# A layernorm, gated MLP and FFT mixer on one core: a new opening order, a second buffer for the squares, and one more unit ahead on the first chunk

## The chip, the core and the metric

The kernel runs on one core of one Trainium2 chip. The time is the device time of one execution in microseconds; the kernel before has a median of 447.81 us over three runs (446.77 to 447.93). All traces are of one execution by the hardware profiler.

## The reference

Three terms are added: x itself, a 2-D Fourier filter of the normalised x, and a gated MLP of the same normalised x. Sizes: 2048 rows, 448 features, 1792 hidden features, all in float32.

```python
xn = (x - mean(x)) / sqrt(var(x) + 1e-5)                  # over the 448 features
A = irfft2(rfft2(xn) * (w_r + 1j * w_i), s=(2048, 448))
gate, up = xn @ W_gate, xn @ W_up                         # 448 x 1792
B = (gate * (gate > 0) * up) @ W_down                     # 1792 x 448
out = x + A + B
```

## The kernel before

Matrix products run in float16 pairs: every operand is split in a high and a low half, and a product is the sum of high-high, high-low and low-high passes. So each weight slab and each activation needs a conversion on ScalarE (`w_hi`, `ln_hi`, `gu_hi`: the high half) and a subtraction on VectorE (`w_lo`, `ln_lo`, `gu_lo`: the remainder). Before a slab (one of gate or up for 128 hidden features: f is the block of features, g is 0 or 1) is converted, it is scaled by a power of two: `w_sq` squares it with a running sum on ScalarE (L186), `w_sum` adds the sums over the partitions on GpSimd (L189), `w_scale` makes the exponent on VectorE (L192, L196), and then come `w_hi` (L681) and `w_lo` (L685). The squares' other output goes into a scratch tile named junk.

The rows of x are taken in 16 blocks of 128, numbered n2, and four blocks form a chunk q (n2 = q + 4 j). The chunks are worked in the order 0, 2, 1, 3. For chunk 0 the normalised blocks are transposed by TensorE (`ln_tp`, L332, with an identity matrix) and evicted into the tile T0 (`ln_ev`, on VectorE or ScalarE); for the others the DMA transposes them (`ln_dma`, L326). One gate/up unit is a pair (f, q): 20 matmuls of 512 columns (`gu_full`, L731), and a half pass for the 64 features that are left over (`gu_half`, L738). The half passes of two units, called mates, stand together in groups of four. A unit's sums are then taken through relu (`gu_relu`, ScalarE, L768), product (`gu_times`, VectorE, L772), `gu_hi` and `gu_lo`. PSUM has two buffers for units, so a unit can open when the product of the last but one is done. After all units of a group of five, five or four f on one chunk, four down products (`dn_mm`, L799) add up their part for its four blocks.

Meanwhile the Fourier transform runs as background work: a list `bg` of pieces, each with an estimated cost on VectorE, which a planner spreads over the units. `PE_US`, `fl`, `bf`, `il` and `V_US` hold the costs, `took` the length of a unit, `fixed` what a unit's own work costs VectorE, and `room` how much background a unit may take; the share is solved so that all fits. `t_ninth` copies leftover rows of T into the tile Tl (L348, L349), and the transform's first matmuls read both (`f_dft`, L361).

The first 45 us, called the opening, are not planned: the table `OPENING` names pieces in order, and each engine takes its part in that order. Of the names: lx and ly load a block of x, lw the next weight slab, lwd a slab of W_down, st, sq and rs make the statistics and the reciprocal root (A for blocks 0 and 4, B for 8 and 12, C for chunk 2), xn, hi, lo, cp normalise and split, tpA and tpB transpose, vev and aev evict, dm is a DMA transpose, wsq, par, wsc, whi, wlo prepare slabs, hh, lh, hl are unit 0's matmuls on half a chunk (256 columns), gu a slab's 20 or 10 matmuls, hp the half passes, re, tm, gh, gl a unit's way out, wd.. the same for W_down. warm and kw are pads: matmuls on a zeroed tile that do no work. All DMAs of this part are issued by SP in its order; SP waits with each for the landing of the one eight places before.

Of the kernel before, what the change touches and what calls it, by code (L numbers as in the profile page):

```python
# [25 lines left out]
NWARM = 19  # L26
# [4 lines left out]
lx0 lx4 lw lid lw lx8 lx12 lw lw lw lw lx2 lx10 lx6 lx14 lwd0 lwd1 lwd2 lwd3 lwd4 warm st0 st4 sqA rsA hi4  # L31
xn4 xn0 wsqW0g0 cp4 st8 hi0 parW0g0 st12 wsqW0g1 cp0 tpA0 lo0 tpA4 kw1 wscW0g0 sqB tpB0 kw6 parW0g1 wsqW1g0
rsB whiW0g0 vevB0 lo4 wsqW1g1 xn12 tpB4 kw3 hi8 parW1 wscW0g1 xn8 whiW0g1 cp8 vevA0 vevA4 hi12 tpA8 vevB4
hh10 hh00 lo8 wsqW2g1 cp12 tpA12 hl00 lo12 aevA12 tpB8 aevA8 hl10 wloW0g0 lw aevB8 tpB12 wscW1 lh00 aevB12
wloW0g1 lw lfd hh01 hh11 whiW1g0 st2 lh01 lh10 whiW1g1 hl01 wloW1g0 lw hl11 wsqW2g0 wloW1g1 lw ly0 ly4 ly8
ly12 lh11 wsqW3g0 st10 parW2 hp0 st14 wsqW3g1 gu1g0 st6 wdq0 parW3 wscW2 sqC wscW3 whiW2g0 rsC gu1g1 re0
wloW2g0 whiW3g1 tm0 whiW2g1 xn6 wsqW4g0 xn2 gu2g0 wloW2g1 hi2 re1 xn10 gh0 wloW3g1 whiW3g0 tm1 gu2g1 wdq1
wloW3g0 hi10 xn14 lo2 hi14 hi6 cp14 hp2 wsqW4g1 cp2 lo6 gu3g0 cp10 dm2 lo14 re2 parW4 wdq2 cp6 wscW4 tm2
whiW4g0 dm14 lo10 wdq4 gu3g1 wloW4g0 gh1 dm10 gl0 whiW4g1 gl1 dm6 gu4g0 re3 wloW4g1 wdq3 tm3 wdp gh3
wdsc gh2 gu4g1 gl2 wdh1 wdh2 wdl1 wdh0 wdl2 hp4 gl3 re4 wdh3 tm4 wdl0 gh4 wdh4 gl4 wdl3 wdl4  # L40
# [4 lines left out]
SQ = 2.0 ** -16  # L45
# [37 lines left out]
def _constants():  # L83
# [55 lines left out]
    ident = np.eye(128, dtype=np.float16)  # L139
    return dict(ident=ident, c_fd=c_fd, c_fm=np.ascontiguousarray(c_fm), c_im=c_im, c_row=c_row,  # L140
# [4 lines left out]
def tile_gfnet_reglu(ctx: ExitStack, tc: tile.TileContext, x, xr, wgu, wd, wf, ident, c_fd, c_fm, c_im, c_row, c_id,  # L145
# [39 lines left out]
    def squares(src, acc):  # L185
        A.activation(mt([128, 512], BF16, "junk")[:, 0:src.shape[-1]], src, AF.Square, scale=SQ, accum_out=acc)  # L186
# [18 lines left out]
    id_t = ft([128, 128], F16, "id_t")  # L205
# [10 lines left out]
    def load_xr(n2):  # L216

        xr_b[n2] = free.pop(0)
        xr_t[n2] = xr_b[n2].rearrange("p g c k -> p (g c k)")[:, 0:D]
        nc.sync.dma_start(xr_t[n2], xrv[:, n2, :])  # L220
# [36 lines left out]
    def ln_sd(q, js=(0, 1, 2, 3)):  # L257
        w = ft([128, 5, 4], F32, "rs", 3)
        n = len(js)
        rst[q, js[0]] = w[:, :, 0:n], mv[q][:, js[0]:js[-1] + 1, :]  # L260
        A.activation(w[:, 0, 0:n], rst[q, js[0]][1][:, :, 1], AF.Sqrt, bias=eps)

    def ln_rstd(q, js=(0, 1, 2, 3), bias=False):
        w, m = rst[q, js[0]]
        sd, r0, t, r, nm = (w[:, i] for i in range(5))
        V.reciprocal(r0, sd)
# [61 lines left out]
    def ln_tp(n2, tiles):  # L328
        if n2 not in tp:
            tp[n2] = fx().bitcast(F16).rearrange("p (a b) -> p a b", b=128)  # L330
        for a in tiles:
            P.transpose(tp[n2][:, a, :], tt[n2][:, a, :], id_t)  # L332
# [395 lines left out]
    def gu_full(f, q, gs, cs, start, stop, seq=SEQ):  # L728
        for g in gs:
# [4 lines left out]
    def gu_half(f, q, g, start, prev):  # L734
# [3 lines left out]
        m = P.matmul(hps[f, q][:, g, 0:512], wt[f, g][rows, 7, :], Tq[q][rows, b, :], start=start, stop=not start).ins  # L738
# [35 lines left out]
    def gu_hi(f, q):  # L774
        ht[f, q] = mt([128, 2, 512], F16, "h", NR + 2)
# [61 lines left out]
    PE_US = {"f_dft": 0.6, "f_sdft": 1.14, "i_sdft": 0.65, "i_ddft": 0.6, "row_dft": 0.2}  # L837
# [4 lines left out]
    def ln_chunk(q):  # L842
        for j in range(4):
            add(0.79, ln_stats, q, j)
# [3 lines left out]
        for t in range(4 + 2):  # L848
            for st, (c, fn) in reversed(list(enumerate(((0.0, ln_norm), (0.78, ln_lo), (0.0, ln_dma))))):
# [372 lines left out]
```

## Time and profile before

| | |
|---|---|
| median of 3 runs | 447.81 us (446.77 to 447.93) |
| the profiled execution | 447.5 us |
| its span, first to last instruction | 445.7 us |
| TensorE, VectorE, ScalarE, GpSimd busy | 438.1, 386.9, 187.0, 27.7 us |
| DMA, mean | 89 GB/s |
| first gate/up matmul | 14.36 us |
| first down matmul | 43.30 us |

In the rows of the profile, L731 is line 731 of the kernel, "out<-in" are tiles by the program's names without buffer numbers, and "x20" is a count. In the timeline the first number is the start in us, the second the length, and the brackets hold the idle time of the engine before it and who ended it. PEld is the loading of weights for TensorE, which overlaps its matmuls; SPq are DMA issues.

### The profile page before, as it was taken

What the parts mean: (1) busy time and instruction counts of PE and PEld (TensorE: products, weight loads), DVE (VectorE), ACT (ScalarE), POOL (GpSimd) and SP (SyncE); (2) the same over time, 40 slices, a digit from 0 to 9 for tenths busy, and PEclk for the clock granted to TensorE, in tenths of its full rate; (3) what the DMA queues carried; (4) which work ended last, traced back from release to release, by engine and by line L of the source; (5) the groups of instructions that cost most, each with busy time, mean ns of one, the idle gap of its engine ahead of it and who ended that gap; (6) DMA issues with size and microseconds to landing.
All of it is one profiled execution on the core that took longest, in us unless ns stands there. A gap on an engine that the chain in (4) does not pass through costs nothing.

```text
span 445.7 us, 7367 instructions
## 1 busy us (share of the span) xinstructions
PE 438.1 (98%) x2625; PEld 219.4 (49%) x2625; DVE 386.9 (87%) x958; ACT 187.0 (42%) x398; POOL 27.7 (6%) x77
## 2 busy tenths in 40 slices
PE   6999999999999999999999999999999999999997
PEld 2644645455445444444444444444454555555654
DVE  5999779786969999899999999999979799699753
ACT  4897263642552975133114354253323134144230
POOL 4220011200100040000000010000000000000000
PEclk9999999999999999999999999999999999999999
DMA  7919995400001272422220210002011211201212
GB/s 249 338 50 252 304 355 106 96 0 17 8 1 48 96 226 80 128 61 83 85 84 2 83 42 1 1 1 73 12 48 47 70 34 56 89 28 53 96 63 82
DMA packets 37756, 39.54 MB, mean 89 GB/s; under 512 B 16550, under 2 KB 33624, under 8 KB 37720
## 3 DMA queue, kind: packets, MB, share of 16 engines
q1 hardware_dynamic: 37720, 39.09, 28.3%
q8 instruction: 20, 0.33, 0.3%
q14 instruction: 16, 0.13, 0.1%
HBM read 24.38 MB, written 3.67 MB: 63 GB/s over the span
## 4 chain that ended last, share of the span: by engine, by line
PE 79%; DVE 9%; DMA 5%; ACT 3%; issue 1%; SPq 1%; DVEq 0%; ACTq 0%
PE gu L731 44%; PE dn L799 22%; PE gu L738 3%; PE fx L630 2%; PE fx L649 2%; PE fx L361 2%; PE fx L398 2%; DMA wf<-in_wf 1%; DMA sw<-y 1%; DMA y<-in_xr 1%; ACT junk L186 1%; PE dn L819 1%; ACT wt L681 1%; PE gu L819 1%; DVE wt L685 1%
## 5 line engine op out<-in xcount | busy, mean ns | idle before, releaser
L731 PE MATMUL gu<-T,wt 128*128 128x512 f16 (+1 forms) x1140 | 255.0, 375 | 0.0
L731 PEld LDWEIGHTS <-wt 128*128 128x128 f16 x1140 | 108.7, 98 | 128.7 <-issue 8.9
L799 PE MATMUL dn<-wdt,h 128*128 128x448 f16 x624 | 127.6, 353 | 0.1
L799 PEld LDWEIGHTS <-h 128*128 128x128 f16 x624 | 60.2, 98 | 57.7 <-issue 0.8
L768 ACT ACTIVATE g<-gu 128x512 f32<-128x512 f32 x56 | 33.0, 590 | 82.4 <-PE gu L738 55.6
L776 ACT ACTIVATE h<-g 128x512 f16<-128x512 f32 x56 | 35.1, 628 | 76.8 <-DVE g L772 73.8
L772 DVE SCALAR_TENSOR_TENSOR g<-gu,g 128x512 f32<-128x512 f32 x56 | 38.3, 684 | 4.2 <-ACT g L768 4.1
L780 DVE TENSOR_TENSOR h<-g,h 128x512 f16<-128x512 f32 x56 | 38.3, 685 | 3.7 <-ACT h L776 3.4
L805 DVE SCALAR_TENSOR_TENSOR xy<-dn,dsc,xy 128x448 f32<-128x448 f32 x44 | 29.9, 679 | 6.3 <-PE dn L799 6.2
L614 ACT ACTIVATE vt<-y,fsc 128x456 f16<-128x456 f32 x16 | 10.8, 673 | 26.1 <-PE fx L630 13.3
L654 DVE SCALAR_TENSOR_TENSOR xy<-fx,fsc,xy 128x448 f32<-128x448 f32 x16 | 10.8, 680 | 11.8 <-PE fx L649 11.7
L681 ACT ACTIVATE wt<-wst,wsc 128x512 f16<-128x512 f32 x28 | 19.2, 715 | 3.8 <-DVE wsc L196 3.8
L685 DVE SCALAR_TENSOR_TENSOR wt<-wst,wsc,wt 128x512 f16<-128x512 f32 x28 | 20.5, 747 | 0.1
L189 POOL PARTITION_ALL_REDUCE wm<-wm x15 | 7.8, 518 | 179.6 <-ACT junk L186 175.5
L186 ACT ACTIVATE junk<-wst 128x512 bf16<-128x512 f32 x28 | 17.5, 624 | 1.0 <-DMA wst<-in_wgu 0.7
L738 PE MATMUL gu<-T,wt 64*128 64x512 f16 x112 | 17.0, 381 | 0.2 <-DVE wt L685 0.2
L535 DVE TENSOR_TENSOR y<-y,sw 128x228 f32<-128x228 f32 x32 | 12.5, 390 | 5.0 <-DMA sw<-y 4.9
L405 DVE TENSOR_TENSOR y<-y,y 128x456 f32<-128x456 f32 x22 | 13.8, 629 | 1.7 <-DMA row<-y 1.4
L392 DVE TENSOR_TENSOR Xh<-X,Xh 128x456 f16<-128x456 f32 x16 | 10.0, 628 | 5.6 <-ACT Xh L389 5.5
L404 DVE TENSOR_TENSOR y<-y,y 128x456 f32<-128x456 f32 x22 | 13.9, 630 | 0.3
L389 ACT ACTIVATE Xh<-X 128x456 f16<-128x456 f32 x16 | 9.3, 578 | 10.1 <-DVE X L387 8.9
L630 PE MATMUL fx<-im,vt 128*128 128x128 f16 x192 | 13.4, 219 | 0.0
(130 smaller groups left out, 479.0 us busy)
## 6 DMA issues: line engine op xcount, KB each, us to landing
sw<-y SPq DMA_DIRECT2D x64, 112.2 KB
wst<-in_wgu SPq DMA_DIRECT2D x28, 256.0 KB
wf<-in_wf SPq DMA_DIRECT2D x16, 228.0 KB
y<-in_xr SPq DMA_DIRECT2D x16, 224.0 KB
xy<-in_x SPq DMA_DIRECT2D x16, 224.0 KB
out<-xy SPq DMA_DIRECT2D x15, 224.0 KB
wdst<-in_wd SPq DMA_DIRECT2D x14, 224.0 KB
fm<-in_c_fm SPq DMA_DIRECT2D x4, 256.0 KB
```

What stands on the lines that cost most here:

```text
L186: A.activation(mt([128, 512], BF16, "junk")[:, 0:src.shape[-1]], src, AF.Square, scale=SQ, accum_out=acc)
L630: P.matmul(o, v[:, h, w], m[:, c, :], start=(i == 0), stop=(i == 2), skip_group_check=True)
L681: A.activation(w[:, 0:4, :], wst[f, g], AF.Copy, scale=wsc[f, g])
L685: V.scalar_tensor_tensor(w[:, 4:8, :], st, sc, w[:, 0:4, :], op0=OP.mult, op1=OP.subtract)
L731: last["P"] = P.matmul(hps[f, q][:, g, cs], wt[f, g][:, a, :], Tq[q][:, b, cs], start=(start and i == 0), stop=(stop and i == len(seq) - 1 ...
L738: m = P.matmul(hps[f, q][:, g, 0:512], wt[f, g][rows, 7, :], Tq[q][rows, b, :], start=start, stop=not start).ins
L768: last["A"] = A.activation(g1s[f, q], hps[f, q][:, 0, :], AF.Relu, scale=2.0 ** -22).ins
L772: last["V"] = V.scalar_tensor_tensor(g1, hps[f, q][:, 1, :], 2.0 ** -22, g1, op0=OP.mult, op1=OP.mult).ins
L776: A.activation(ht[f, q][:, 0, :], g1s[f, q], AF.Copy)
L780: V.tensor_tensor(h[:, 1, :], g1s.pop((f, q)), h[:, 0, :], op=OP.subtract)
L799: last["P"] = P.matmul(ps[:, 0:D], ht[f, q][:, a, js], wdt[f][:, b, :], start=(i == 0), stop=(i == n - 1)).ins
L805: last["V"] = V.scalar_tensor_tensor(xy[:, n2, :], dps[n2][:, 0:D], dsc[:, g:g + 1], xy[:, n2, :], op0=OP.mult, op1=OP.add).ins
```

## The change

It rewrites the table of the opening, and what goes with it:

- The order. Four weight slabs instead of two are loaded ahead of x's third block, and slab W01 is squared first. The two transposed blocks of the second half come after the first matmuls of units 0 and 1. Unit 1 is also done in halves (ah, bh, ch).
- A sixth unit. The unit (f = 5, chunk 0) is taken out of the second group's place and done in the opening, as the mate of unit 4; its output has a tile of its own, h0, until the group's down product. The mates after it shift by one.
- The identity comes with block 4 in one load (`xi`), and the DMA of its own goes. The third block that TensorE transposes uses a PSUM buffer of the down products.
- The squares' scratch tile has two buffers.
- The root and the reciprocal become one function, Abs_reciprocal_sqrt, and VectorE's reciprocal goes.
- The pads: 15, 1, 8 and 1 instead of 19, 1, 6 and 3; VectorE clears their tile instead of GpSimd.
- The planner's costs are lower, and a unit whose fixed work exceeds its share passes the lack on to the units ahead of it (`rooms`). `c_fm` is loaded not before unit 6.

On ScalarE, at the start of the program, before. wst_124, 127, 131 and 133 are the slabs W00, W01, W10 and W11; L186 squares, L300 converts a block of x, L261 is the root, L681 scales a slab:

```order
L300 ACTIVATE tt0_103<-y1_71,rs_179 128x448
L186 ACTIVATE junk_190,wm_189<-wst_124 128x512
L300 ACTIVATE tt1_104<-y0_70,rs_179 128x448
L186 ACTIVATE junk_202,wm_189<-wst_127 128x512
L261 ACTIVATE rs_220<-mv_174,eps_95 128x2
L186 ACTIVATE junk_235,wm_234<-wst_131 128x512
L681 ACTIVATE wt_242<-wst_124,wsc_217 128x512
L186 ACTIVATE junk_247,wm_234<-wst_133 128x512
L300 ACTIVATE tt2_105<-y2_72,rs_220 128x448
L681 ACTIVATE wt_264<-wst_127,wsc_260 128x512
```

The same place now, with wst_159, 161, 165 and 167 for W00, W01, W10 and W11, and L685 for the scaling:

```order
L303 ACTIVATE tt0_102<-y0_70,rs_131 128x448
L305 ACTIVATE tt1_103<-y1_71 128x448
L186 ACTIVATE junk_176,wm_175<-wst_161 128x512
L186 ACTIVATE junk_191,wm_175<-wst_159 128x512
L186 ACTIVATE junk_196,wm_195<-wst_165 128x512
L186 ACTIVATE junk_198,wm_195<-wst_167 128x512
L685 ACTIVATE wt_211<-wst_161,wsc_207 128x512
L685 ACTIVATE wt_229<-wst_159,wsc_226 128x512
L342 ACTIVATE T0_62<-fx_171 128x5x128
L265 ACTIVATE rs_246<-mv_124,eps_95 128x2
```

The four squares now stand together ahead of all scalings, and the conversion of the third block of x has moved behind four scalings.

On ScalarE around the relu of unit 2 (L768 before, g1_513), before:

```order
L768 ACTIVATE g1_457<-gu_380 128x512
L776 ACTIVATE h_460<-g1_431 128x512
L681 ACTIVATE wt_463<-wst_311,wsc_412 128x512
L186 ACTIVATE junk_476,wdm_403<-wdst_145 128x448
L302 ACTIVATE tt1_104<-y14_84 128x448
L302 ACTIVATE tt2_105<-y15_85 128x448
L302 ACTIVATE tt3_106<-y12_82 128x448
L186 ACTIVATE junk_492,wm_440<-wst_364 128x512
L768 ACTIVATE g1_513<-gu_444 128x512
```

The same now (L776 is the relu, g1_446 that of unit 1 and g1_525 that of unit 2):

```order
L776 ACTIVATE g1_446<-gu_272 128x512
L265 ACTIVATE rs_461<-mv_359,eps_95 128x4
L186 ACTIVATE junk_464,wm_463<-wst_456 128x512
L186 ACTIVATE junk_466,wdm_392<-wdst_371 128x448
L685 ACTIVATE wt_472<-wst_368,wsc_469 128x512
L186 ACTIVATE junk_512,wm_463<-wst_458 128x512
L303 ACTIVATE tt0_102<-y8_78,rs_461 128x448
L776 ACTIVATE g1_525<-gu_474 128x512
```

Between the two relus now stand the squares of unit 5's slabs, the root of chunk 2 and one conversion, where three conversions of chunk 2 and unit 0's own way out stood; these follow later.

On SP, the transposes of chunk 2 (into T2) and the copies of chunk 0's leftover rows (into Tl0), before:

```order
L1056 DMA fd_t_101<-in_c_fd 128x912
L226 DMA wst_355<-in_wgu 128x512
L226 DMA wst_364<-in_wgu 128x512
L214 DMA xy_61<-in_x 128x448 x4
L326 DMA_TRANSPOSE T2_63<-tt0_103 128x8x128
L326 DMA_TRANSPOSE T2_63<-tt2_105 128x8x128
L326 DMA_TRANSPOSE T2_63<-tt1_104 128x8x128
L326 DMA_TRANSPOSE T2_63<-tt3_106 128x8x128
```

And now:

```order
L329 DMA_TRANSPOSE T2_63<-tt1_103 128x8x128
L329 DMA_TRANSPOSE T2_63<-tt2_104 128x8x128
L329 DMA_TRANSPOSE T2_63<-tt0_102 128x8x128
L213 DMA xy_61<-in_x 128x448
L329 DMA_TRANSPOSE T2_63<-tt3_105 128x8x128
L244 DMA fm_696<-in_c_fm 128x1024
L1067 DMA fd_t_100<-in_c_fd 128x912
L224 DMA y15_85<-in_xr 128x448
L224 DMA y16_86<-in_xr 128x448
L224 DMA y2_72<-in_xr 128x448
L224 DMA y1_71<-in_xr 128x448
L352 DMA Tl0_66<-T0_62 16x512 x3
```

A load of x now stands ahead of the last transpose, and the load of c_fd, which stood before all of them, has come between the transposes and the copies into Tl0.

The core of the diff:

```diff
-NWARM = 19
+NWARM = 15
 OPENING = """
-lx0 lx4 lw lid lw lx8 lx12 lw lw lw lw lx2 lx10 lx6 lx14 lwd0 lwd1 lwd2 lwd3 lwd4 warm st0 st4 sqA rsA hi4
...
+lx0 st0 lx4 st4 sqA rsA hi0 warm tpA0 xn4 xn0 lw lw lo0 lw lw hx4 kw1 tpA4 wsqW0g1 cp0 tpB0 lx8 lo4 lx12 cp4
...
-        A.activation(mt([128, 512], BF16, "junk")[:, 0:src.shape[-1]], src, AF.Square, scale=SQ, accum_out=acc)
+        A.activation(mt([128, 512], BF16, "junk", 2)[:, 0:src.shape[-1]], src, AF.Square, scale=SQ, accum_out=acc)
...
+        if n2 == 4:
+            t = mt([128, 512], F32, "g1", 3)
+            nc.sync.dma_start(t, xi)
+            xr_t[n2], state["id"] = t[:, 0:D], t[:, D:].bitcast(F16)
+            return
...
-        A.activation(w[:, 0, 0:n], rst[q, js[0]][1][:, :, 1], AF.Sqrt, bias=eps)
+        A.activation(w[:, 0, 0:n], rst[q, js[0]][1][:, :, 1], AF.Abs_reciprocal_sqrt, bias=eps)
...
-        V.reciprocal(r0, sd)
...
+            t = fx() if len(tp) != 2 else psum.tile([128, 512], F32, name="dn", bufs=2)
...
-        ht[f, q] = mt([128, 2, 512], F16, "h", NR + 2)
+        ht[f, q] = mt([128, 2, 512], F16, "h", NR + 2) if (f, q) != (NR, CHUNKS[0]) else mt([128, 2, 512], F16, "h0")
...
-    PE_US = {"f_dft": 0.6, "f_sdft": 1.14, "i_sdft": 0.65, "i_ddft": 0.6, "row_dft": 0.2}
+    PE_US = {"f_dft": 0.58, "f_sdft": 0.58, "i_sdft": 0.7, "i_ddft": 0.57, "row_dft": 0.1}
...
-    bf = (1.26, 2.04, 2.04, 2.04, 1.56, 2.04, 2.04, 2.04)
+    bf = (1.09, 1.71, 1.71, 1.71, 1.23, 1.71, 1.71, 1.71)
...
+    ahead = ("gu", 1, groups[1][0], CHUNKS[0])
+    gseq.remove(ahead)
+    gseq.insert(len(groups[0]), ahead)
...
-        sched(gus[5 + 2 * c], load_fm, q)
+        sched(max(gus[5 + 2 * c], len(groups[0]) + 1), load_fm, q)
...
-        A.activation(mt([128, 1], F32, "root"), eps, AF.Sqrt)
-        G.memset(warm, 0.0)
+        A.activation(mt([128, 1], F32, "root"), eps, AF.Abs_reciprocal_sqrt)
+        V.memset(warm, 0.0)
...
-    took = lambda u: 4.55 if u[0] == "gu" else 0.56 * len(groups[u[1]])
-    V_US = {"w_scale": 0.33, "w_lo": 0.75, "wd_scale": 1.5, "wd_lo": 0.68}
+    took = lambda u: 4.62 if u[0] == "gu" else 0.56 * len(groups[u[1]])
+    V_US = {"w_scale": 0.3, "w_lo": 0.67, "wd_scale": 1.4, "wd_lo": 0.59}
...
-        c = 1.37 if units[i][0] == "gu" else 0.68
+        c = 1.21 if units[i][0] == "gu" else 0.6
...
-    def room(i, share):
-        return max(0.0, share * took(units[i]) - fixed(i))
+    def rooms(share):
+        r, short = [0.0] * len(units), 0.0
+        for i in reversed(range(len(units))):
+            v = share * took(units[i]) - fixed(i) + short
+            r[i], short = max(0.0, v), min(0.0, v)
+        return r
```

More of the change, by code (lines that the diff above doesn't have):

```diff
@@ L732, in gu_full, with gu_half @@
                                      start=(start and i == 0), stop=(stop and i == len(seq) - 1)).ins
-    def gu_half(f, q, g, start, prev):
+    def gu_half(f, q, g, start, prev, stop):
         rows, b = TOP[g]
-        m = P.matmul(hps[f, q][:, g, 0:512], wt[f, g][rows, 7, :], Tq[q][rows, b, :], start=start, stop=not start).ins
+        m = P.matmul(hps[f, q][:, g, 0:512], wt[f, g][rows, 7, :], Tq[q][rows, b, :], start=start, stop=stop).ins
         if "opened" in state:
@@ L756, in gu_halves @@
     def gu_halves(f, q, mate):
-        gu_open(*mate)
+        fresh = mate not in hps
+        if fresh:
+            gu_open(*mate)
         m = last["P"]
@@ L1016, in gslot @@
         return gus[n] if n >= 0 else -1
-    for f in groups[1] + groups[2]:
+    for f in groups[1][1:] + groups[2]:
         s = first[f]
@@ L1028, in tile_gfnet_reglu @@
     for i in range(8):
-        sched(gslot(first[groups[1][0]], 14 - i // 2), load_wn)
+        sched(gslot(first[groups[1][1]], 14 - i // 2), load_wn)
     for c, q in enumerate(CHUNKS[1:]):
@@ L1136, in tile_gfnet_reglu @@
         need = sum(c - m * p for c, p, _, _ in bg)
-        lo, hi = (m, hi) if sum(room(i, m) for i in range(RAMP, last_gu)) < need else (lo, m)
+        lo, hi = (m, hi) if sum(rooms(m)[RAMP:last_gu]) < need else (lo, m)
     load[0] = hi
+    room = rooms(hi)
     anchors, act_anchors = [last["V"]], [last["A"]]
@@ L1145, in after @@
             yield
-    for i, u in list(enumerate(units))[len(groups[0]):-4]:
+    for i, u in list(enumerate(units))[len(groups[0]) + 1:-4]:
         is_gu = u[0] == "gu"
```

82 lines of the change are left out of this document (44 added, 38 removed).

## The prediction

> **What bounds the kernel now.** I read the page first (busy time by engine), then what TensorE waited for, then the chain of waits, and last the timeline of the first 50 us, where the change is.
>
> ```profile
> span 445.7 us, 7367 instructions
> PE 438.1 (98%) x2625; PEld 219.4 (49%) x2625; DVE 386.9 (87%) x958; ACT 187.0 (42%) x398; POOL 27.7 (6%) x77
> PE dn L1054 <- POOL warm L1111: 3.6, 1, 3.6
> PE fx L332 <- ACT wt L681: 0.5, 1, 0.5
> PE gu L738 <- DVE wt L685: 0.2, 1, 0.2
> 15.34 0.44 PE gu L731 x4
> 38.50 0.54 PE gu L738 x4
> 76.03 4.32 PE gu L731 x20
> ```
>
> The three PE rows with "<-" are all of TensorE's waits that the profile names: after 20 us it waits for nobody. The last three rows are pieces of the chain: a 256-wide gate/up matmul takes 0.44 / 4 = 0.109 us, a 512-wide one 4.32 / 20 = 0.216 us, a group of four half passes 0.54 us. So from about 20 us on the kernel is the plain sum of TensorE's stream. A change of order can win only by starting that stream earlier, or lose by new waits. The profiled execution took 447.5 us, 1.8 us beside its span of 445.7; the median of the runs is 447.81 us, 0.3 us above it.
>
> In the opening TensorE waits for ScalarE, which is nearly full:
>
> ```profile
> 10.00:20.00 10.00, 9.30 (x87) 6.65 (x86) 9.64 (x32) 9.17 (x20) 1.91 (x6) 1.00 0.96 357
> 20.00:30.00 10.00, 10.00 (x50) 4.14 (x47) 9.19 (x26) 9.32 (x23) 0.93 (x5) 1.00 0.29 94
> 13.39 0.72 ACT L681 ACTIVATE wt<-wst,wsc 128x512 f16<-128x512 f32 x1 [0.55 <-DVE wsc L196]
> 14.15 0.18 PEld L332 LDWEIGHTS <-tt 128*128 128x128 f16 x3 [0.95 <-ACT wt L681]
> 14.36 0.81 PE L731 MATMUL gu<-T,wt 128*128 128x256 f16 x6
> 38.97 4.49 PE L731 MATMUL gu<-T,wt 128*128 128x512 f16 x20
> ```
>
> The two stage rows give, after their length, the busy time of TensorE, its weight loads, VectorE, ScalarE and GpSimd: ScalarE has 9.17 and 9.32 of 10 us. The first gate/up matmul is at 14.36. At 38.97 the five opening units of chunk 0 are done, with three groups of half passes.
>
> **The change, part by part.** Its yardstick is the moment at which six units of chunk 0 are done. Before, that moment would be 38.97 + 4.32 (the sixth unit's twenty matmuls) = 43.29. All other work of TensorE stays, but for 20 more, shorter matmuls since unit 1 is cut in halves: 40 x 0.109 - 20 x 0.216 = +0.04, and 25 pad matmuls for 29.
>
> Loads and normalisation:
>
> ```profile
> 4.88 0.29 ACT L261 ACTIVATE rs<-mv,eps 128x2 f32<-128x2 f32 x1 [2.64 <-DVE mv L253]
> 5.20 0.17 DVE L266 RECIPROCAL rs<-rs 128x2 f32<-128x2 f32 x1 [0.36 <-ACT rs L261]
> 5.40 0.16 DVE L267 SCALAR_TENSOR_TENSOR rs<-mv,rs 128x2 f32<-128x2 f32 x1
> 6.19 0.76 ACT L300 ACTIVATE tt<-y,rs 128x448 f16<-128x448 f32 x1 [1.01 <-DVE rs L271]
> 6.85 0.62 ACT L186 ACTIVATE junk<-wst 128x512 bf16<-128x512 f32 x1
> 7.47 0.75 ACT L300 ACTIVATE tt<-y,rs 128x448 f16<-128x448 f32 x1
> 8.42 0.63 DVE L250 BATCH_NORM_STATS2 bst<-y 128x6 f32<-128x448 f32 x1 [1.42 <-DMA y<-in_xr]
> 9.67 2.83 SPq L236 DMA_DIRECT2D wdst<-in_wd  x5
> ```
>
> Without the reciprocal (5.40 - 5.20 = 0.20) ScalarE's first conversion starts at 5.99 instead of 6.19; it occupies 6.85 - 6.19 = 0.66, the second, a copy of the same size, about 0.6 (an estimate from the first), so ScalarE is free for squares at 7.25. The first square needs the fourth transfer in the new queue. Before, x's third block ended its wait at 8.42 with 1,216 KB queued up to it (three blocks of 128 x 448 floats, 224 KB each, two slabs of 128 x 512, 256 KB each, and the identity, 32 KB); the five issues from 9.67 each follow a landing of 224 to 256 KB, so (2.83 - 0.33) / 4 = 0.63 us each, some 390 KB per us. Now 992 KB lead up to that slab: 8.42 - 224 / 390 = 7.85 at the latest, 7.25 at the earliest; I take 7.85, the end that a row gives. x's third block itself comes at 9.7, but by then four slabs' work is at hand, which covers it. The memset of the pads goes to VectorE, idle until 3.27, and costs nothing; the pads end before 10.1, under the wait for the first slab.
>
> The squares:
>
> ```profile
> 18.87 0.63 ACT L186 ACTIVATE junk<-wst 128x512 bf16<-128x512 f32 x1
> 19.63 0.63 ACT L186 ACTIVATE junk<-wst 128x512 bf16<-128x512 f32 x1
> 16.09 1.68 ACT L338 ACTIVATE T<-fx 128x384 f16<-128x384 f16 x3 [0.22 <-PE fx L332]
> 15.78 0.29 PE fx L332 x5
> 23.43 1.32 ACT L681 ACTIVATE wt<-wst,wsc 128x512 f16<-128x512 f32 x2
> 22.95 0.58 ACT L768 ACTIVATE g<-gu 128x512 f32<-128x512 f32 x1
> 23.83 0.69 DVE L772 SCALAR_TENSOR_TENSOR g<-gu,g 128x512 f32<-128x512 f32 x1
> 24.43 0.93 DVE L293 TENSOR_SCALAR y<-y,mv,rs 128x448 f32<-128x448 f32 x2
> ```
>
> A square followed by another kind of work holds ScalarE 0.62 us (6.85 to 7.47), one followed by a square 0.76 (18.87 to 19.63). I put the 0.14 down to the single junk buffer, and let it go with two. Four squares from 7.85 then end at 10.33; the first scaling starts there, and TensorE follows 14.15 - 13.39 = 0.76 later, as at 13.39 above. The first gate/up matmul moves **from 14.36 to about 11.1**.
>
> From there ScalarE sets the pace. Up to unit 2's relu its new order holds 9 scalings (0.62, from the row of two), 8 squares of slabs (0.62), 3 of W_down (0.57, the estimate 0.62 x 448 / 512 rounded up), 3 conversions (0.65), 3 evictions (1.6 together, as the row of three), 2 roots (0.30) and 2 relus (0.6): 17.6 us, and 0.2 of waiting. So relu 2 starts at 10.33 + 17.8 = 28.1. Its product on VectorE stands behind two normalisations (0.93 - 0.51 = 0.42 each) that wait for the fifth pair's sums, and starts at 29.5. TensorE gets the buffer 0.73 later, at 30.24, having waited 0.68. Then come three slabs (6.48), a wait of 0.13, half passes (0.53), two slabs (4.32): the sixth unit ends at **41.7**. From the other side: 11.08 + 28.7 of work (80 x 0.109, 80 x 0.216, three groups of half passes, 16 transposes at 0.29 / 5, a pad) + 1.9 of waits = 41.7; 0.6 of these waits lie before 15 us, 1.3 at products that free buffers. Stepped through in the same way, the order of before ends at 39.24 where the profile has 38.97, so this working is 0.27 late. The gain is 43.29 - 41.7 + 0.27 = 1.9; the first down matmuls take 0.1 of it, waiting for the third W_down remainder. Remaining: **1.8 us**.
>
> Work that was hidden and is moved:
>
> ```profile
> 30.71 5.43 SPq L326 DMA_TRANSPOSE T<-tt  x4
> 37.76 1.85 SPq L220 DMA_DIRECT2D y<-in_xr  x4
> 39.66 1.88 SPq L348 DMA_DIRECT2D Tl<-T  x3
> 49.04 0.21 PE L361 MATMUL fx<-fd_t,Tl 128*128 128x114 f16 x1
> 176.17 2.85 DMA sw<-y
> ```
>
> In SP's queue the last transpose of chunk 2 now stands behind a load, and by the same stepping its tile is ready at about 39.3; it is issued until 39.3 + 5.43 / 4 = 40.7, the six loads behind it until 43.5 (1.85 / 4 = 0.46 each), the four Tl copies until 45.9 (about 0.6 each). By the row of 2.85, the nearest one of copies within the core, they land at 48.2; TensorE asks for them at 49.04 + 1.4 (more work ahead of it) - 1.8 = 48.6. Cover 0.4 us; if it is gone, up to 1 us is lost. The transposes were issued until 30.71 + 5.43 = 36.1 and used at 38.5 (the half passes above) with no wait, so they land 2.4 us after that at the latest: 43.1 now, for matmuls at 41.4 + 0.1 + 1.5 (eight down matmuls, about 0.19 each by their 448 columns) = 43.0.
>
> The planner's table (background costs down by a sixth, fixed costs by a tenth) moves no work in or out. I take it at 0, bounded below by -0.3 (no more waits are there to be saved) and above by the third rival. The two reciprocals that go later are under VectorE's other work.
>
> Sum: 447.5 - 1.8 = 445.7 for an execution like the profiled one, and with the median 0.3 above it **446.0 us**. If the slabs land early enough (first square at 7.25), about 0.4 better.
>
> **The rivals.**
>
> *The second buffer frees nothing.* That the edit doesn't do what it says: the 0.14 may be the accumulator's read and not the buffer. Eight of the squares before relu 2 stand directly ahead of another: 8 x 0.14 = 1.1 us back, 447.1. For it: only one stage shows the 0.76. Against: other neighbours show 0.62 with the same read. Chance 0.17.
>
> *The clock.*
>
> ```profile
> 8.68 0.15 PEld L1054 LDWEIGHTS <-warm 128*128 128x128 f16 x1 [0.28 <-issue]
> 8.98 0.96 PEld L1054 LDWEIGHTS <-warm 128*128 128x128 f16 x5 [0.15 <-issue]
> ```
>
> The pads pass one every 0.15 + 0.28 = 0.43 us, from 8.98 on every 0.2: 5 us after their start at 3.6 the array runs twice as fast. Between 10.1 and 14 TensorE now stands idle about a third of the time. If that throws it back for another 5.1 us, half of these are lost, 2.5 us less the 0.6 of waits: 447.9. Against: the weight load at 14.15 followed 0.95 us without one, and the matmuls at 15.34 run at 0.109. Chance 0.05. The Trainium skill (TensorE: Matmul & The Clock Gate, Part 1) has a window of about 3.4 us without work halve the clock; by that rule the gaps here are too short, the trace agrees as far as it goes, and the sum stays.
>
> *The planner overfills VectorE: slower.*
>
> ```profile
> 200.00:250.00 50.00, 49.90 (x246) 22.63 (x245) 48.86 (x105) 15.03 (x37) 0.00 (x0) 1.00 0.21 62
> 250.00:300.00 50.00, 50.00 (x251) 22.96 (x250) 49.13 (x116) 21.41 (x49) 4.17 (x6) 1.00 0.08 23
> ```
>
> VectorE idles 1.14 + 0.87 = 2.0 us in these 100. If the new table brings more than 2.0 us more work there, TensorE waits for the excess at buffers that products and down evictions free; the sign turns from 3.8, the verdict from 5.1. At 6 us, a shift of 6%, it costs 4: 450.0. For it: costs are changed by up to a sixth, unevenly. Against: the share is solved so that all fits, and TensorE waited nowhere there. Chance 0.11.
>
> *The root in another function set.* ScalarE begins with a table load of 1.28 us:
>
> ```profile
> 0.74 1.28 ACT L1110 ACT_TABLE_LOAD   x1 [0.74 <-PEq L1210]
> ```
>
> Were two more needed around each of the three roots of the opening, 6 x 1.28 = 7.7 us would fall on the engine that sets the pace: 453.7. But the order of the new program holds one load. Chance 0.01. The Trainium skill (ScalarE: Activation LUTs, What ACT_TABLE_LOAD costs) adds a drain to each switch of set; by that page the loss would be about twice as large, an estimate.
>
> **How the numbers follow.** The forecast has 0.66, with its own range from 444.7 (early slabs, and the cover holds) to 446.9 (1 us lost at Tl). A measurement of this kernel tells about 0.3%, 1.3 us, from no change. Of the 0.66, 0.06 fall short of that. So faster 0.60; no change 0.06 + 0.17 + 0.05 = 0.28; slower 0.11 + 0.01 = 0.12. The range 444.7 to 447.7 takes in the forecast and the second buffer's rival, and leaves out the ends below, the clock and the two slower cases.
>
> **What would show it.** Right: the first gate/up matmul between 10.5 and 11.2; squares in a row 0.62 apart; relu 2 at about 28; no named wait of TensorE above 0.7 us after 20 us; the sixth unit of chunk 0 done near 41.5. Wrong: squares at 0.76 (second buffer), pads or 256-wide matmuls at twice their time after 10 us (clock), waits of TensorE between 200 and 300 us (planner), or a wait at the Tl matmul near 48.6. If TensorE's named waits after 45 us sum to over 1 us, the claim that only the opening counts is wrong.

## The result and the profile after

The changed kernel is slower: 449.93 us in the median of 13 executions (447.43 to 452.18), against 447.11 for the kernel before on the same chips (13 executions, 446.44 to 448.04). The ratio is 1.0054, with an interval of 1.0033 to 1.0074. The forecast of 446.0 us, with a range up to 447.7, was wrong, and on the wrong side.

Two things make up the difference: new waits of TensorE, and in most executions a stretch at a lower TensorE clock. The profiled execution had the full clock (1.00) throughout and took 448.04 us (span 446.1), about 0.5 us more than the profiled execution of before (447.5). Four of the 13 were of this kind (447.43 to 448.04). The other nine had a mean granted clock of 0.996 or 0.991 of full speed and took 449.62 to 452.18.

The opening does what the prediction said, and more. ScalarE in the new opening (timeline of the profile after; the last brackets hold the idle time ahead of an instruction and who ended it):

```profile
5.98 0.76 ACT L303 ACTIVATE tt<-y,rs 128x448 f16<-128x448 f32 x1 [0.82 <-DVE rs L274]
...
7.12 0.61 ACT L186 ACTIVATE junk<-wst 128x512 bf16<-128x512 f32 x1
...
7.73 0.61 ACT L186 ACTIVATE junk<-wst 128x512 bf16<-128x512 f32 x1
...
9.57 1.32 ACT L685 ACTIVATE wt<-wst,wsc 128x512 f16<-128x512 f32 x2
```

The first square starts at 7.12, the next 0.61 later, the scalings at 9.57. TensorE follows (same view, after; the rows are picked from 8 to 82 us):

```profile
10.32 1.90 PE L737 MATMUL gu<-T,wt 128*128 128x256 f16 x11
...
29.30 6.63 PE L737 MATMUL gu<-T,wt 128*128 128x512 f16 x30 [0.36 <-DVE g L780]
...
40.83 1.68 PE L807 MATMUL dn<-wdt,h 128*128 128x448 f16 x8
43.03 2.75 PE L737 MATMUL gu<-T,wt 128*128 128x512 f16 x12 [0.52 <-DVE h L788]
...
48.07 0.72 PE L365 MATMUL fx<-fd_t,T 128*128 128x114 f16 x11
49.74 0.21 PE L365 MATMUL fx<-fd_t,Tl 128*128 128x114 f16 x1 [0.95 <-DMA Tl<-T]
...
76.40 2.32 PE L737 MATMUL gu<-T,wt 128*128 128x512 f16 x10
80.10 2.32 PE L737 MATMUL gu<-T,wt 128*128 128x512 f16 x10 [1.38 <-DVE g L780]
```

Six units of chunk 0 are done at 40.83, where the kernel before would have had them at 43.29: 2.46 us won. (In the profiled executions of e1 and e15, the same kernel, they are done at 40.99 and 41.01.) Then TensorE stops three times. Eight down matmuls of 0.19 end at 42.35, and the next starts at 43.03: 0.68 lost. Eleven of 0.05 end at 48.62, the next starts at 49.74: 1.12. Ten of 0.216 end at 78.56, the next starts at 80.10: 1.54. Together 3.34 against 2.46. The kernel before loses about 0.4 us between 195 and 208 us that the new one doesn't (21 down matmuls take 4.33 us there, against 3.99 at 0.19 each), so 0.5 is left at the end.

Who is late shows in SP's queue (timeline, after):

```profile
34.09 4.97 SPq L329 DMA_TRANSPOSE T<-tt  x3
39.11 0.57 SPq L213 DMA_DIRECT2D xy<-in_x  x1
39.79 1.25 SPq L329 DMA_TRANSPOSE T<-tt  x1
...
46.00 0.59 SPq L353 DMA_DIRECT2D Tl<-T  x1
...
65.21 1.96 SPq L213 DMA_DIRECT2D xy<-in_x  x4
...
68.67 1.69 SPq L544 DMA_DIRECT2D row<-y  x2
70.53 5.51 SPq L329 DMA_TRANSPOSE T<-tt  x4
76.14 1.58 SPq L544 DMA_DIRECT2D row<-y  x2
```

The first stop waits for chunk 2's last transpose, issued until 41.04 behind a load of x. VectorE's L788, which the row names, ended at 42.50, and in e13 below the same matmul didn't wait for it. In e1, e5, e7, e12 and e15 the row of this stop names other instructions, but each time the matmul starts 2.2 to 2.3 us after SP is done with the last transpose (2.0 here). The second stop waits for the last copy into Tl, issued at 46.00 and landed at 49.47 by the chain. The third is indirect, as VectorE's timeline shows (after):

```profile
72.75 0.63 DVE L408 TENSOR_TENSOR y<-y,y 128x456 f32<-128x456 f32 x1
78.07 0.63 DVE L409 TENSOR_TENSOR y<-y,y 128x456 f32<-128x456 f32 x1 [4.69 <-DMA row<-y]
...
79.36 0.68 DVE L780 SCALAR_TENSOR_TENSOR g<-gu,g 128x512 f32<-128x512 f32 x1
```

L409 overwrites in place a block whose row is being copied (`row<-y`, L544). That copy stands in SP's queue behind four transposes, which began at 70.53, behind two other row copies and loads that SP issued until 68.3. VectorE stands for 4.69 us, and the product that frees TensorE's buffer (79.36) is behind it. The same places in the kernel before (SP, before):

```profile
68.46 4.05 SPq L326 DMA_TRANSPOSE T<-tt  x3
72.61 1.58 SPq L540 DMA_DIRECT2D row<-y  x2
```

The four transposes were issued until 72.51 before and until 76.04 now, and the row copies behind them start at 72.61 and 76.14: 3.53 us late.

Why is SP so late there? Three stretches of before, then of after (length, busy time of TensorE, weight loads, VectorE, ScalarE, GpSimd; clock, DMA share, GB/s):

```profile
22.00:34.00 12.00, 12.00 (x58) 5.17 (x57) 10.89 (x32) 11.05 (x26) 2.47 (x9) 1.00 0.24 68
34.00:50.00 16.00, 16.00 (x97) 7.90 (x96) 12.17 (x28) 8.61 (x17) 0.45 (x1) 1.00 0.90 252
50.00:70.00 20.00, 20.00 (x121) 10.15 (x119) 16.67 (x56) 10.51 (x22) 3.03 (x8) 1.00 0.88 316
```

```profile
22.00:34.00 12.00, 11.64 (x55) 4.95 (x54) 11.39 (x33) 11.60 (x28) 3.37 (x7) 1.00 0.01 2
34.00:50.00 16.00, 14.51 (x83) 6.84 (x82) 10.90 (x25) 7.19 (x14) 0.74 (x5) 1.00 0.91 215
50.00:70.00 20.00, 20.00 (x129) 10.28 (x126) 17.87 (x56) 10.79 (x22) 3.08 (x8) 1.00 0.99 353
```

From 22 to 34 us the new kernel moves 2 GB/s, since SP waits there at the first transpose of chunk 2 with the loads behind it. Such a gap is not new: before, SP waited at the same place until 30.71, and by 30 us both kernels had moved as much (227 GB/s on the mean before, 229 now). But chunk 2's remainders, for which SP waits there, come later from VectorE in the new opening. So the first transpose is issued at 34.09, and the last leaves SP at 41.04, where it was 36.14 before (30.71 + 5.43). All that stands behind in the queue is late by that.

Added up from the start, the new kernel is 0.4 MB ahead at 22 us (312 GB/s on the mean against 292); it moves 0.8 MB less from there to 34 and 0.6 MB less from 34 to 50, and is then 0.9 MB behind. At the 353 GB/s of the full stretch that follows, 0.9 MB are an estimated 2.7 us. That is the greater part of the 3.53; the rest is not accounted for.

### The profile page after: what moved, and what is told of

Read it like the earlier page. It is cut to its first block, busy times and chain, and to the rows that moved or that the text cites. A ratio compares the mean times of both kernels' runs of the same rounds, so it can differ in the third digit from the quotient of the medians.

```text
span 446.1 us, 7389 instructions
## 1 busy us (share of the span) xinstructions
PE 438.0 (98%) x2641; PEld 220.7 (49%) x2641; DVE 390.0 (87%) x955; ACT 183.8 (41%) x398; POOL 28.2 (6%) x76
## 4 chain that ended last, share of the span: by engine, by line
PE 84%; DVE 6%; SPq 3%; ACT 3%; issue 2%; DMA 2%; POOL 0%; ACTq 0%; DVEq 0%
PE gu L737 45%; PE dn L807 26%; PE gu L744 3%; PE fx L634 2%; PE fx L653 2%; PE fx L365 2%; PE fx L402 2%; SPq L329 1%; ACT junk L186 1%; PE dn L827 1%; DVE tt L320 1%; DVE wt L689 1%; DMA Tl<-T 1%; PE gu L827 1%; DVE bst L254 1%
## 5 line engine op out<-in xcount | busy, mean ns | idle before, releaser
L737 PEld LDWEIGHTS <-wt 128*128 128x128 f16 x1160 | 111.0, 98 | 129.5 <-issue 9.8
L776 ACT ACTIVATE g<-gu 128x512 f32<-128x512 f32 x56 | 33.3, 594 | 118.1 <-PE gu L744 71.4
L788 DVE TENSOR_TENSOR h<-g,h 128x512 f16<-128x512 f32 x56 | 38.2, 684 | 4.9 <-ACT h L784 4.6
L685 ACT ACTIVATE wt<-wst,wsc 128x512 f16<-128x512 f32 x28 | 19.0, 712 | 10.2 <-DVE wsc L196 10.2
L409 DVE TENSOR_TENSOR y<-y,y 128x456 f32<-128x456 f32 x22 | 13.9, 630 | 5.3 <-DMA row<-y 4.7
L186 ACT ACTIVATE junk<-wst 128x512 bf16<-128x512 f32 x28 | 17.2, 618 | 0.0
L189 POOL PARTITION_ALL_REDUCE wm<-wm x15 | 6.9, 468 | 150.1 <-ACT junk L186 143.9
L431 DVE SCALAR_TENSOR_TENSOR y<-y,y 128x456 f32<-128x456 f32 x20 | 12.6, 630 | 0.5
```

Source lines behind the costliest of these rows:

```text
L186: A.activation(mt([128, 512], BF16, "junk", 2)[:, 0:src.shape[-1]], src, AF.Square, scale=SQ, accum_out=acc)
L685: A.activation(w[:, 0:4, :], wst[f, g], AF.Copy, scale=wsc[f, g])
L737: last["P"] = P.matmul(hps[f, q][:, g, cs], wt[f, g][:, a, :], Tq[q][:, b, cs], start=(start and i == 0), stop=(stop and i == len(seq) - 1 ...
L776: last["A"] = A.activation(g1s[f, q], hps[f, q][:, 0, :], AF.Relu, scale=2.0 ** -22).ins
L788: V.tensor_tensor(h[:, 1, :], g1s.pop((f, q)), h[:, 0, :], op=OP.subtract)
```

## The experiments

Ratios are to the kernel before on the same chip. The expectations name their theories as follows. Theory one is that named waits of TensorE make up the loss (in e5, that VectorE is stuck behind the late row copy), theory two that the clock does. Theory A, from e7 on, goes further: SP's queue and the transfers are late after 40 us because loads stand behind the transposes of chunk 2, and the waits follow from that. Its rivals are the planner's new table (theory B), and that each wait is a fault of its own.

**e1_again and e15_again: the changed kernel, nothing edited.**

> The changed kernel once more, nothing edited. Two parts of the loss are to be told apart. Theory one (waits): even with the clock at 1.00 throughout, the 2.4 us won in the opening are given back by three named waits of TensorE, near 42 us (0.5), 49 us (0.95) and 80 us (1.4): such executions take 447.4 to 448.1 us. Theory two (clock): in about two executions of three the mean clock is 0.996, about 3.5 us at half rate, and they take 449.6 to 451.0. If the profiled execution is one of those, its stages show in which stretch the clock was below 1.00: 5 to 14 us (thin opening), 46 to 50 us (the wait for Tl) or 78 to 82 us (the wait for a unit buffer). A rival: the clock figure is noise of the records and the longer executions have another cause; then the matmuls' spacing is the same in both kinds of execution.

448.57 us (447.50 to 450.45, 10 executions), ratio 1.0036 (1.0021 to 1.0051); three of ten at 0.995 or 0.996. The profiled one took 449.11 at full clock, 1.0 above the range of theory one: the three stops named 1.5 (at 44.13), 0.6 (Tl) and 1.7 us (the unit buffer), where the first profile had 0.5, 0.95 and 1.4. The waits alone vary that much from one execution to the next.

> The changed kernel once more, nothing edited, for the record of an execution whose clock falls back. If the stretch with the wait for a unit buffer does it, the half-rate stretch of 3.4 us begins between 79 and 85 us and the window of 3.4 us before it has TensorE busy for less than about 0.35 of its time; if the opening or the Tl wait does it, it begins before 20 us or at 46 to 56 us. If the profiled execution is at 1.00 again, this stays open.

448.79 us, ratio 1.0023 (1.0013 to 1.0033), one of ten at 0.996. The profiled one was at 1.00 again, 449.14 us with 1.4 us at the first stop, none at Tl and 2.5 at the unit buffer. Where the changed kernel itself falls to half rate has stayed open.

**e2_tl_fd: the first two waits taken away.**

```diff
-... cp8 wsqW3g1 lx14
+... cp8 wsqW3g1 lx14 lfd
-... gh3 ly8 dm14 ... gh5 lfd gl4 gl5
+... gh3 dm14 ... gh5 gl4 gl5 ly8
+    add(0.0, t_ninth, 0)
     for j in range(4):
         add(0.0, load_xr, CHUNKS[2] + 4 * j)
-    add(0.0, t_ninth, 0)
```

> Only SP's order is changed: the load of c_fd goes right behind x's block 14, x's eighth stored block goes to the end of the opening, so that the last transpose of chunk 2 is issued 0.6 us sooner, and the Tl copies of chunk 0 go ahead of the four loads of chunk 1. Theory one (waits): the waits at 42 us (0.5 to 0.7) and at 49 us (0.95) go, the one at 80 us (1.4) stays; executions at full clock take 446.4 to 447.0 instead of 447.8. If the stretch at 46 to 50 us is what throws the clock back, all executions show 1.00; if it is the stretch at 78 us or the opening, about two in three still show 0.996. Rival: something else is late in the place of Tl (other loads now behind it), and the time stays at 447.8 and above.

447.88 us (446.50 to 449.71), ratio 1.0014 (0.9998 to 1.0029): about 1 us above what was expected. The waits at 42 and 49 us were gone (that down group ran into the next matmul at 42.49, Tl's matmul came at 48.10), and the third grew. What TensorE waited for in this kernel (total, times, longest):

```profile
PE gu L737 <- DVE g L780: 3.8, 2, 3.4
```

TensorE came 1.6 us sooner to a copy that was later still: SP issued the second pair of row copies at 77.28, not at 76.14. Three in twelve executions were at 0.996.

**e3_row_act and e4_all: the row copies issued by ScalarE.**

```diff
-last["R"] = nc.sync.dma_start(row[...], cur["s1", j, par][64:65]).ins
+last["R"] = nc.scalar.dma_start(row[...], cur["s1", j, par][64:65]).ins
```

> Only the 32 small copies of the spectrum's row (row from y) are issued from ScalarE's queue instead of SP's, so that they don't stand behind four transposes of 1.4 us each at 70.5 us. Theory one (waits): VectorE's 4.7 us wait for the row copy before line 409 goes, with it TensorE's 1.4 us at 80 us; executions at full clock take 446.3 to 446.7 instead of 447.8; the waits at 42 and 49 us stay. If the wait at 78 us is what throws the clock back, all executions show 1.00 and the median falls by 3.5 us, to about 446.5; if not, two in three still show 0.996. Rival (the planner's new numbers overfill VectorE there, the copy is not the cause): the wait at 80 us stays, with another name.

> Both edits of the two kernels before together. Theory one (waits): TensorE has no named wait over 0.3 us after 31 us; executions at full clock take 444.8 to 445.4, 1.7 to 2.3 us below the kernel of before. If the clock falls back because of the waits at 46 to 50 or 78 us, all executions are at 1.00 and the median is there; if the thin opening does it (5 to 14 us), two in three still take 2.2 us more, about 447.2. Rival: new waits come up later for the saved ones, since VectorE is nearly full from 200 to 300 us, and the time at full clock stays above 446.5.

Both were worse: 450.76 (ratio 1.0080, 1.0056 to 1.0103) and 451.12 (1.0083, 1.0065 to 1.0102). ScalarE's queue now stood still at the copy (timeline of ScalarE, e3_row_act):

```profile
64.67 0.57 ACT L393 ACTIVATE Xh<-X 128x456 f16<-128x456 f32 x1
69.82 1.32 ACTq L544 DMA_DIRECT2D row<-y  x1
71.19 0.63 ACT L784 ACTIVATE h<-g 128x512 f16<-128x512 f32 x1 [5.95 <-issue]
```

For 5.95 us nothing left ScalarE, and TensorE waited 1.9 us for an eviction. By the chain of waits the copy was let go when a load of x landed at 69.75. So this doesn't test the theory as meant; it shows that a late DMA held up the other queue as well once it stood there. But e4's record shows the clock fall back (stretches of e4_all, columns as above; 0.50 is half rate):

```profile
70.62:74.03 3.41, 1.11 (x10) 0.55 (x9) 3.19 (x9) 2.98 (x7) 2.69 (x8) 1.00 0.85 277
74.03:80.86 6.83, 5.99 (x26) 2.68 (x26) 4.22 (x9) 1.48 (x3) 0.11 (x1) 0.50 0.95 156
80.86:84.27 3.41, 3.41 (x22) 1.70 (x20) 3.41 (x12) 1.43 (x3) 0.00 (x0) 1.00 0.17 39
```

**e5_join and e6_tl_fd_join: VectorE no longer held by the copy.**

```diff
+        if (src, j, par) == ("s1", 0, 0):
+            t = free.pop()
+            V.tensor_tensor(t, a, b, op=OP.add)
+            V.tensor_tensor(a, a, b, op=OP.subtract)
+            free.insert(len(free) // 2, b)
...
```

> The changed kernel, with one edit: the first butterfly of chunk 0 writes its difference into the other of its two inputs, the one whose row was copied early, so that VectorE no longer waits there for the row copy that stands behind four transposes in SP's queue. Theory one (VectorE stuck behind that copy): VectorE's wait of 4.7 us goes, with it TensorE's 1.4 us at 80 us; executions at full clock take 446.3 to 446.7 instead of 447.4 to 448.0; the waits at 42 us (0.5) and 49 us (0.6 to 0.95) stay. Clock: in the record of an earlier kernel the clock went to half from 74.0 to 80.9 us, behind a stretch of 3.4 us in which TensorE was idle for most of 3 us; if the wait at 78 us is what does it in the changed kernel, all executions here show 1.00 and the median falls by about 3 us, to 446.5; if the opening does it, two in three still show 0.996. Rival: the butterflies run earlier, and another buffer or the next product is late by as much.

> The edit of the kernel before, and the two of e2_tl_fd (load of c_fd early, last transpose of chunk 2 sooner, Tl copies ahead of the four loads of chunk 1). If the three waits are the whole of the loss, TensorE has no named wait over 0.3 us after 31 us, and the offset won in the opening (2.4 us at 24 us of TensorE's work) is still 2.0 to 2.4 at 100 us: 444.6 to 445.3 us, all executions at 1.00. If the opening is what throws the clock back, two in three take 2 us more. Rival: what is saved is lost again between 80 and 200 us at other buffers, and the time is 446 or more.

e5: 447.96 us, ratio 1.0019 (1.0010 to 1.0028), all eleven executions at 0.999 or 1.00. The clock part came out, the time didn't: the first stop was 1.1 us here, and TensorE now also stopped a few matmuls on, at the Tl of chunk 2, the next thing in SP's queue (TensorE, e5_join):

```profile
82.09 0.27 PE L365 MATMUL fx<-fd_t,Tl 128*128 128x114 f16 x2 [1.47 <-DMA Tl<-T]
```

e6 took 450.52 (1.0066, 1.0047 to 1.0084), five us above the expectation, with five of six executions at 0.996. The idea that the three waits are faults of their own fell here: with all three mended, TensorE met the same late queue 2.59 us early and in one piece, and the clock fell back. TensorE's timeline and the stretches of e6_tl_fd_join:

```profile
82.16 0.37 PE L365 MATMUL fx<-fd_t,Tl 128*128 128x114 f16 x2 [2.59 <-DMA Tl<-T]
```

```profile
78.72:82.14 3.42, 0.85 (x4) 0.20 (x2) 1.76 (x6) 1.65 (x3) 0.00 (x0) 1.00 0.14 34
82.14:85.56 3.42, 3.40 (x10) 1.39 (x11) 2.70 (x12) 3.09 (x7) 0.66 (x3) 0.50 0.02 5
85.56:89.00 3.44, 3.44 (x19) 1.31 (x18) 3.34 (x9) 2.10 (x5) 0.96 (x4) 1.00 0.35 79
```

**e7_oldcost and e8_newcost: the planner's table alone.** e7 is the changed kernel with all costs and the `room` of before; e8 is the kernel of before with the new ones.

```diff
-    bf = (1.09, 1.71, 1.71, 1.71, 1.23, 1.71, 1.71, 1.71)
+    bf = (1.26, 2.04, 2.04, 2.04, 1.56, 2.04, 2.04, 2.04)
...
```

> The changed kernel with the planner's table of before (all its costs, fixed costs and the old rule for room); the opening is the new one. Theory A (the late transfers make the row copy late, whatever the planner): VectorE still waits 3 us or more for it and TensorE over 1 us near 78 us; time as the changed kernel, 447.5 to 450. Theory B (the new table put the in-place difference right ahead of the product that frees TensorE's buffer): with the old table a product and a statistics step stand ahead of it, TensorE's wait at 78 us is under 0.3, and executions take 446.4 to 446.9, all at 1.00. The waits at 42 and 49 us stay in both.

> The kernel of before, with nothing but the planner's new table (costs, fixed costs, room). Theory B (the table by itself brings the wait): TensorE waits over 0.5 us at a buffer that a product frees, between 60 and 90 us, and the time is 448 or more. Theory A (it needs the late transfers too): no such wait over 0.3; 447.0 to 447.4, as before, or up to 0.4 less, since the 0.35 us that before loses near 204 us are not there with the new table.

e7: 449.05 us, 1.0050 (1.0032 to 1.0067), all at 0.999 or 1.00. The wait near 78 us was gone, as theory B said, because a product and a statistics step stood ahead of L409, though VectorE still waited 2.65 us there for the row copy. But TensorE waited 0.9 us at 43 us, 0.5 between 84 and 100 and 1.3 between 190 and 200, so the time was no better, 2 us above what theory B said. The second pair of row copies was issued at 76.39, as late as with the new table. e8: 446.83 us, 0.9990 (0.9981 to 0.9998). In the old order the new table is worth 0.36 us. The table decides who meets the late copy, not that it is late.

**e9_early, e10_early_tl, e11_early_tl_join: the loads ahead of the transposes.** Six loads go into the gap, four of them (chunk 2's blocks of x) from the planner's hands:

```diff
-... re1 st6 lx10 st10 ...
+... re1 st6 lx10 ly8 ly2 ly10 ly6 ly14 lfd st10 ...
-... gh3 ly8 dm14 ... gh5 lfd gl4 gl5
+... gh3 dm14 ... gh5 gl4 gl5
-        for j in range(4):
+        for j in range(4 if c else 0):
             sched(gus[7 + 5 * c], load_x, q + 4 * j)
```

> The changed kernel with six loads that SP issued after 39 us (x's eighth stored block of the opening, the four of chunk 2, c_fd) put ahead of the four transposes of chunk 2, into the 12 us from 22 to 34 us in which no transfer ran. Nothing else is edited. Theory A (SP's queue and the transfers are late after 40 us because the new opening left these loads behind the transposes): the second four transposes start at 67 to 68.5 us instead of 70.5, the row copy no longer holds VectorE for more than 2 us, TensorE's three waits (42, 49 and 80 us) shrink to under 0.6 together, and executions take 444.7 to 445.6, all at 1.00. Theory B (the planner's new numbers): the wait near 78 us stays over 1 us. Rival: the six loads now delay the transposes of chunk 2, and the wait at 42 us grows.

> The kernel before, and the Tl copies of chunk 0 ahead of chunk 1's four loads. Theory A: as the kernel before, but no wait at Tl near 48 us at all; 444.5 to 445.3, all at 1.00. If four loads of about 0.5 us each behind the copies matter more than the copies, the start of chunk 1 is late and the time is 445.5 or more.

> The kernel before, and the butterfly of e5_join, which doesn't write over the row that is being copied. Theory A: once SP is on time the copy holds up nobody, so this edit is worth nothing: within 0.4 us of e10_early_tl. Theory B (the order on VectorE is the fault by itself): it is worth 1 us or more here too.

446.08 (0.9980, 0.9970 to 0.9989), 446.34 (0.9986, 0.9977 to 0.9995) and 445.79 us (0.9979, 0.9963 to 0.9994): the first versions below the kernel before. The three waits of the changed kernel were gone in e9 (VectorE still waited 2.3 us for the row copy), but about 1 us was missing to the expectation. TensorE's waits in e9_early:

```profile
PE gu L737 <- ACT wt L685: 1.7, 1, 1.7
```

The six loads stood ahead of the last two weight slabs, and TensorE waited for a scaled slab at 30.68. Tl's copies ahead of chunk 1's loads (e10) changed nothing that can be told. The butterfly (e11) has no wait at the product near 78 us, where e10 had 0.5 us; but e9, without the butterfly, had none there either. By the medians it is worth 0.5, between what the two theories said, and the intervals of the two kernels overlap, so a gain isn't shown. One execution of e11 in nine was at 0.996 (448.37 us), for which no trace shows a cause.

**e13_early2 and e14_early2_all: the same, behind the slabs.**

```diff
-ly0 wscW4 ...
+ly0 ly8 ly2 ly10 ly6 ly14 lfd wscW4 ...
```

> As e9_early, but the six loads stand behind the last two weight slabs of the opening instead of ahead of them. If the late loads are the whole of the loss after the opening, the slabs come as in the changed kernel (no wait for a scaled slab over 0.4 us before 40 us), SP is as early after 55 us as in e9_early, and the time is 0.9 to 1.4 us below e9_early's 446.1: 444.7 to 445.2, all at 1.00. If it stays at 446, the offset of the opening goes at another place.

> The kernel before, with the Tl copies of chunk 0 ahead of chunk 1's four loads and the butterfly of e5_join. From e11_early_tl_join (445.8) less the 0.9 us at the slabs: 444.5 to 445.0, all at 1.00.

e13: 444.93 us (444.71 to 445.99), ratio 0.9950 (0.9936 to 0.9964), all at 1.00: faster than the kernel before (447.57 on this chip) and than the changed kernel (e15: 448.79 on the same chip). TensorE's waits in e13_early2, then its SP queue, VectorE and TensorE at the old places:

```profile
PE dn L1065 <- DVE warm L1125: 1.2, 1, 1.2
PE gu L737 <- DVE g L780: 0.4, 1, 0.4
```

```profile
34.16 6.25 SPq L329 DMA_TRANSPOSE T<-tt  x4
...
67.03 5.51 SPq L329 DMA_TRANSPOSE T<-tt  x4
72.64 1.58 SPq L544 DMA_DIRECT2D row<-y  x2
```

```profile
74.57 0.63 DVE L409 TENSOR_TENSOR y<-y,y 128x456 f32<-128x456 f32 x1 [2.90 <-DMA row<-y]
...
75.86 0.68 DVE L780 SCALAR_TENSOR_TENSOR g<-gu,g 128x512 f32<-128x512 f32 x1
```

```profile
74.69 4.48 PE L737 MATMUL gu<-T,wt 128*128 128x512 f16 x20
79.00 0.26 PE L365 MATMUL fx<-fd_t,Tl 128*128 128x114 f16 x2
```

The 0.4 is the wait at 29.3; after it TensorE waits for nobody. The transposes start at 67.03 instead of 70.53. VectorE still waits for the copy, 2.90 us, but the product is done at 76.5, 0.3 us before TensorE's next unit (74.69 and ten matmuls of 0.216), and TensorE runs through its matmuls and Tl's at 79.00 without a stop. e14 brought 445.67 us (0.9954, 0.9941 to 0.9966), 0.7 above its expectation and no better: with SP on time no gain of its two edits can be told.

So the loads behind the transposes are the whole of the loss after the opening, as far as the two profiles tell: e13's span of 442.9 us is 2.8 below that of before, and that is the 2.4 of its opening (six units done at 40.90) and the 0.4 that before loses near 204 us. Whether earlier transposes, with the loads left behind them, would do as much was not tested.

**e12_junk1: one scratch buffer for the squares.**

```diff
-        A.activation(mt([128, 512], BF16, "junk", 2)...
+        A.activation(mt([128, 512], BF16, "junk", 1)...
```

> The changed kernel with one buffer for the squares' output instead of two. My step (the second buffer lets squares follow each other 0.62 us apart): here they are 0.76 apart again, relu 2 comes about 1 us later, and the six units of chunk 0 end 0.8 to 1.2 us later, at 41.6 to 42.0 us instead of 40.8. The rival of the prediction (the buffer frees nothing): still 0.62 apart, and 40.8.

The squares were 0.73 to 0.76 apart again (ScalarE, then TensorE, e12_junk1):

```profile
7.21 0.61 ACT L186 ACTIVATE junk<-wst 128x512 bf16<-128x512 f32 x1
...
7.94 0.63 ACT L186 ACTIVATE junk<-wst 128x512 bf16<-128x512 f32 x1
...
8.70 0.63 ACT L186 ACTIVATE junk<-wst 128x512 bf16<-128x512 f32 x1
```

```profile
41.20 1.68 PE L807 MATMUL dn<-wdt,h 128*128 128x448 f16 x8
```

The buffer does what I said, but is worth 0.2 to 0.4 us at the sixth unit (41.20 against 40.83 to 41.01 in the three profiles of the changed kernel), not 0.8 to 1.2. The kernel took 449.46 us (1.0050, 1.0032 to 1.0068).

## Why the prediction was wrong

- **The opening: right, and undersized.** Its term was 1.9 us, and it measured 2.46. I took the first square at 7.85, the end that a row gave; it came at 7.12, before the early end of 7.25. The rest followed by the same steps: scalings at 9.57, TensorE 0.75 later at 10.32, a wait of 0.36 for relu 2's buffer where I had 0.68. The 0.1 at the first down matmuls didn't come.
- **The second buffer: right in kind.** That rival falls with e12. Its price of 1.1 us was at least three times too high: the scalings began 0.5 us later there (10.08), and by the sixth unit 0.2 to 0.4 was left.
- **The failed step: "Work that was hidden and is moved".** I followed SP's queue to the Tl copies at 48 us, took the transposes of chunk 2 at about nothing and the copies at "up to 1 us", outside the forecast. Both covers were gone. The transposes were there by 43.0, as worked out, but TensorE already at 42.35, since the opening was faster. The copies landed at 49.5 instead of 48.2: SP had issued them by 46.6 and not 45.9, and the last took 3.47 us from issue to landing where I had used the row of 2.85. That is 1.8 us lost. And I stopped there. My own sum had the transposes leave SP at 40.7 instead of 36.1, so everything behind them 4.6 us late (measured 4.9), and I asked only for the first users. The loads behind carried the delay on to 76 us: the row copy was 3.53 us late, and TensorE lost 1.54 us more. The limit I had set, 1 us of named waits after 45 us, was passed with 0.95 + 1.38.
- **The range.** Its lower end of 444.7 does not follow from its terms: 446.0 less 0.4 for early slabs and 0.3 for the planner is 445.3.
- **The planner: priced right, and not alone.** Taken at 0, bounded at -0.3, it gave -0.36 in the old order (e8; by the interval -0.1 to -0.8). Its rival was placed at 200 to 300 us, where nothing happened; together with the late copy it chose the place of the third wait (e7).
- **The clock: the wrong place.** In no trace did the clock fall back between 10 and 14 us. In e4 and e6 it fell back behind the new waits, which I had not foreseen. In the three sets of the changed kernel 13 of 33 executions were below 0.999. Of the edited versions of it in whose trace TensorE waits for nothing longer than 1.5 us between 70 and 90 us (e5, e7, e9, e10, e11, e13, e14), one execution of 60 was, in e11. That the wait near 78 us is what does it in the changed kernel is inferred from this and from the records of e4 and e6; no execution of its own that lost clock was profiled.

## What to carry to other kernels

A faster opening brings every later consumer forward, so it has to be followed through the transfer queue until that queue is empty, not only to the first use. Compare when each queue is done with its slow pieces, and the bytes transferred, added up from the start, in the old and the new profile: a single stretch with few transfers can mislead, since they may have been done before. What is behind when the transfers become full falls due later, as waits under other engines' names. When a wait is removed and another comes up just behind it, look for the queue that both stand in, and move what is ahead of them.

## What the runs showed of the hardware

TensorE's clock is set in windows of 3.41 us that lie differently in each execution (in the 16 traces that record it the full clock began between 3.9 and 8.9 us, and lasted a whole number of windows). A window need not be idle to be followed by half rate. It fell back behind windows with 0.25 (e6: 0.85 of 3.42) and 0.33 (e4: 1.11 of 3.41) of TensorE busy, and held behind these two of e2_tl_fd and e15_again, at 0.43 and 0.50:

```profile
75.62:79.03 3.41, 1.46 (x7) 0.59 (x6) 0.00 (x0) 0.00 (x0) 0.00 (x0) 1.00 0.73 164
```

```profile
76.93:80.34 3.41, 1.72 (x8) 0.69 (x7) 1.16 (x3) 0.00 (x0) 0.00 (x0) 1.00 0.37 83
```

So where a wait falls decides what it costs. In e4, 2.3 us without matmuls in one window were followed by half rate; a window at half rate loses half of 3.41 us of work, an estimated 1.7 us. e2's wait of 3.4 us was split by a boundary and cost no clock in its profiled execution. The Trainium skill (TensorE: Matmul & The Clock Gate, Part 1), which the prediction drew on, lets half rate follow an idle window; these records put the limit between a third and 0.43 of the window busy, and the measurement decides.
